# Attention and feed-forward on one core: first-layer products of the mean in four pieces, key pieces shared between two engines, first keys loaded ahead of the second weights

## The chip, the cores and the metric

The kernel runs on 1 core of one Trainium2 chip. Its engines work side by side, each through its own list of instructions in order: TensorE (PE, with its weight loads PEld), VectorE (DVE), ScalarE (ACT), GpSimd (POOL) and SyncE (SP), which here issues all DMAs. The metric is the device time of one execution in microseconds (us); lower is better.

## The reference

```python
B, C, Hh, Ww = (4, 128, 384, 32)            # q: (4, 12288, 128), kv: (4, 384, 32, 128)
kv_pool = kv.reshape(B, H // 4, 4, W // 4, 4, C).mean(axis=(2, 4))
k = v = kv_pool.reshape(B, -1, C) @ w_sr     # 768 keys per batch
s = scale * (q @ k.transpose(0, 2, 1))
a = exp(s - s.max(-1)); a /= a.sum(-1) + 1e-09
x = (a @ v).reshape(49152, 128)
h = x @ w_in                                 # 128 -> 2048
out = (h - tanh(h)) @ w_out                  # 2048 -> 128
```

The weights w_in and w_out are float64.

## The kernel before

The work is cut into 96 **groups** of 512 tokens, 24 for each of the 4 batches. The kernel does not compute the softmax directly: it works with the differences from the batch's mean key, for which expansions are exact enough, and a branch behind it computes everything plainly if that does not hold for the inputs.

Per batch, `keys` loads the keys in 12 pieces of 512 KB, sums each window of 16 (on POOL as four folds, L363, or on DVE as one reduction, L369), takes the mean (L391 to L396), shifts the keys by it, and multiplies with w_sr. `about_centre` multiplies the mean with w_in (**first**, L475: 16 products of one column, two passes each), takes h on DVE, and computes there from it, in some twenty short steps on 16 columns (L483 to L515), value, slope and third-order factor of the activation. From these it makes the value (L519), the matrix A of slopes (L602), the scaled w_in (`winr`) and the scaled w_out (`Wr`, by POOL, L607).

Per group, `attention` has 6 score products, in three tiles (L649), their exponentials less 1 and less s (ACT L653, DVE L656, tile r2), the sum of shares (L669), the sum of values (L673, L678), and dl, the result on DVE (L688), rounded on POOL to dr. `feed_forward` has 16 products **forth** (L726, in 8 tiles), a square on ACT and a cube on DVE (L730, L733; for one or two of the 8 tiles a copy on ACT and three steps on POOL, L737 to L744, tile rp) and 16 products **back** (L766) with the straight product (L715) into one accumulator, and ACT's copy with the value added (L772), which is stored.

At the start the float64 weights are turned into float32 by `words_of`: a load, three ACT steps and four DVE steps (L257, L260, L264, L276) for each of 4 parts of w_in and of w_out. `fits` computes at the end the flag for the branch: limits from h and the weights (L797 to L822), then the comparison with the shares (L835 to L852).

PSUM holds a ring of three **big** tiles (scores, forth and some others), one accumulator **acc**, and one **x** bank, which all the small products and the sums of attention take in turn.

The order of every engine's list is fixed when the kernel is built: each operation has a step number (its priority) and an assumed duration, and `Plan.run` places them one after the other in a time of its own; where an engine can begin several, the lowest step goes first. So a changed step or duration moves instructions all through the program.

Of the kernel before, what the change touches and what calls it, by code (L numbers as in the profile page):

```python
# [20 lines left out]
P = 128  # L21
KB = 64
# [124 lines left out]
def attention_then_ffn(ctx: ExitStack, tc: tile.TileContext, q, kv, w_sr, w_in, w_out, out):  # L147
# [18 lines left out]
    BUFS = {"kc": 2, "kvp": 1, "kTr": 2, "vv32": 1, "vvr": 2, "Mn": 2, "A": 2, "Wg": 2, "Wr": 2,  # L166
            "winr": 2, "q": 4, "qr": 3, "E": 2, "r2": 5, "t": 2, "dl": 2, "dr": 2, "u": 3, "r": 4,
            "rp": 2, "rs": 2, "v": 2, "z": 1, "o": 2, "row": 2, "col": 2, "G0": 2, "hb": 2, "W2": 1,
# [51 lines left out]
    WORDS = {"i": ("u", "u", "u", "E"), "o": ("E", "rs", "rs", "z")}  # L220

    def words_of(step, load_step, n, kind):
# [56 lines left out]
        plan.op(load_step, "SP", 0.5, load_words, (), (words,), late=2.0, dma=1.65)  # L279
# [8 lines left out]
    def weights(step, load_step):  # L288
# [3 lines left out]
        for n in range(NW):  # L292
            words_of(step + NW + n, load_step + 1 + n / 8, n, "o")
        for j in range(2):
            turned = f"turned.{j}"
            big(turned, step + 2 * NW + j)
            for k in range(2):
                def turn(j=j, k=k, turned=turned):
                    for f in range(8 * j + 4 * k, 8 * j + 4 * k + 4):
                        PE.matmul(out=plan[turned][:, (f % 8) * P : (f % 8 + 1) * P],  # L300
                                  lhsT=win32[:, f * P : (f + 1) * P], rhs=ident,
                                  start=True, stop=True)

                plan.op(step + 2 * NW + j, "PE", 1.0, turn, (("win32", 2 * j + k), "ident"),
                        ((turned, k),), late=0.2)
# [4 lines left out]
            plan.op(step + 2 * NW + j, "ACT", 1.03, copy, (turned,), (("winT", j),), late=0.1)  # L310
# [29 lines left out]
    def keys(b, s0):  # L340
# [7 lines left out]
        for j in range(NK):  # L348
            gap = 11 if b else 0.1
# [7 lines left out]
            plan.op(s - 8, "SP", 0.5, load, (), (key,), late=2.0, dma=1.65)  # L357
            if b or j % 3 == 2:
# [22 lines left out]
        for x, at in ((pc, s0), (pm, s3), (p4, s4)):  # L381
            bank(x, "x", at)
        big(pk, s1)
# [25 lines left out]
        def product():  # L409
            for c in range(2):  # L410
                PE.matmul(out=plan[pk][:, c * G : c * G + KH], lhsT=wsr,
                          rhs=plan[kvp][:, c * KH : (c + 1) * KH], start=True, stop=True)
# [5 lines left out]
        def product_by_key():  # L418
            for n in range(KT):
# [7 lines left out]
        def small_values():  # L427
            V.tensor_scalar(out=plan[vvr].rearrange("p k c -> p (k c)"), in0=plan[pv][:, 0:K],  # L428
                            scalar1=1.0 / (W * K), scalar2=None, op0=ALU.mult)
# [16 lines left out]
        plan.op(s1, "PE", 1.2, product, ("wsr", kvp), (pk,), late=0.2)  # L446
        plan.op(s1, "ACT", 0.9, copy_keys, (pk,), (kTr,), late=0.1)
        plan.op(s2, "PE", 1.75, product_by_key, ("wsr", kvp), (pv,), late=0.2)
        plan.op(s2, "ACT", 0.85, copy_values, (pv,), (vv32,), late=0.1)
        plan.op(s2, "DVE", 0.9, small_values, (pv,), (vvr,))  # L450
# [4 lines left out]
    def about_centre(b, s0):  # L455
# [11 lines left out]
        by = 4 if b else 1  # L467
        s1, s2, s3, s4, s5 = (s0 + n * by for n in range(1, 6))
        bank(ph, "x", s0 if b else s0 - 9.5)
        bank(pg, "x", s2 if b else s5 + 2)  # L470
        bank(pa, "x", s5 if b else s1 - 0.5)

        def first(n):
            for f in range(4 * n, 4 * n + 4):
                PE.matmul(out=plan[ph][:, f : f + 1], lhsT=win32[:, f * P : (f + 1) * P],  # L475
                          rhs=plan[cen], start=True, stop=True)
# [4 lines left out]
        def take():  # L481
            h, z = x(0), x(1)
            V.tensor_scalar(out=h, in0=plan[ph][:, 0:FT], scalar1=1.0, scalar2=None, op0=ALU.mult)  # L483
            V.tensor_tensor(out=z, in0=h, in1=h, op=ALU.mult)

        def first_order():
            h, z, p, g0, g1, a3, slope, y, inv = (x(n) for n in range(9))
            V.tensor_scalar(out=p, in0=z, scalar1=17.0 / 315, scalar2=-2.0 / 15, op0=ALU.mult,
# [28 lines left out]
        def value(n):  # L517
            for f in range(4 * n, 4 * n + 4):
                PE.matmul(out=plan[pg][:, 0:1], lhsT=wout32[:, f], rhs=x(3)[:, f : f + 1],  # L519
                          start=(f == 0), stop=(f == FT - 1))  # L520

        def copy_value():
            V.tensor_scalar(out=plan[G0], in0=plan[pg][:, 0:1], scalar1=1.0, scalar2=None,  # L523
                            op0=ALU.mult)

        for n in range(4):
            plan.op(s0, "PE", 1.1, partial(first, n), (cen, ("win32", n)), ((ph, n),), late=0.2)
        plan.op(s0, "DVE", 0.5, take, (ph,), (hb,))
        plan.op(s0 + 0.1, "DVE", 1.6, first_order, (hb,), (hb, gg))
        plan.op(s0 + 0.2, "DVE", 1.6, slopes_of, (hb,), (hb, iv))  # L530
        plan.op(s0 + 0.3, "DVE", 1.6, third_order, (hb,), (hb, ("stat", b), a3s))
        for n in range(4):
            plan.op(s2 if b else s5 + 2, "PE", 1.0, partial(value, n), (gg, ("wout32", n)), (pg,), late=0.2)
        plan.op(s2, "DVE", 0.12, copy_value, (pg,), (G0,))
        NW, FW = 4, FT // 4
        if b:
# [5 lines left out]
            plan.op(s0 + 1, "SP", 0.5, store_inverse, (iv,), (f"inverse.{b}",), late=2.5, dma=0.1)  # L542
            for j in range(2):
# [16 lines left out]
                plan.op(s0 + 1, "SP", 0.5, load_inverse, (f"inverse.{b}",), (ir,), late=2.5, dma=2.2)  # L560
                plan.op(s1 + j, "DVE", 2.2, scaled, (ir, "win32"), ((winr, j),), port=True)
        else:
            for j in range(2):
                pw = f"pw.{b}.{j}"
                big(pw, s1 + j * by / 2)
                for k in range(2):
                    dg = f"dg.{b}.{j}.{k}"
                    sb(dg, "Wg", [P, FW, C], step=s1 + j * by / 2 + k / 4)
# [14 lines left out]
                    plan.op(s1 + j * by / 2, *(("POOL", 1.25) if j else ("DVE", 1.1)), diagonal, (iv, "ident"), (dg,), port=True)  # L583
                    plan.op(s1 + j * by / 2, "PE", 0.9, scaled, (dg, "winT"), ((pw, k),), late=0.2)
# [4 lines left out]
                plan.op(s1 + j * by / 2, "ACT", 1.03, copy_scaled, (pw,), ((winr, j),), late=0.1)  # L589
        for n in range(NW):  # L590
            wg = f"wg.{b}.{n}"
            fs = slice(n * FW, (n + 1) * FW)
            sb(wg, "Wg", [P, FW, C], step=s3 + n / 4)

            def by_first(n=n, wg=wg, fs=fs):
                by = x(4)[:, fs].unsqueeze(2).to_broadcast([P, FW, C])
                (PL if b or n % 2 else V).tensor_tensor(out=plan[wg], in0=wout32[:, fs], in1=by, op=ALU.mult)

            def slopes(n=n, wg=wg):
                for k in range(FW):  # L600
                    f = n * FW + k
                    PE.matmul(out=plan[pa][:, 0:P], lhsT=winT[:, f], rhs=plan[wg][:, k],  # L602
                              start=(f == 0), stop=(f == FT - 1))

            def by_third(fs=fs):
# [3 lines left out]
            plan.op(s3 + n / 4, *(("POOL", 1.25) if b or n % 2 else ("DVE", 1.15)), by_first,  # L609
                    (gg, ("wout32", n)), (wg,), port=True)  # L610
            plan.op(s5, "PE", 1.1, slopes, (wg, "winT"), (pa,), late=0.2)
            plan.op(s4 + n / 4, "POOL", 1.25, by_third, (a3s, ("wout32", n)), ((Wr, n),))

        def copy_slopes():
            A.copy(out=plan[Am], in_=plan[pa][:, 0:P])

        plan.op(s5, "ACT", 0.3, copy_slopes, (pa,), (Am,), late=0.1)

    def attention(g, s0):
# [17 lines left out]
        plan.op(s0 - 10, "SP", 0.5, load_q, (), (qs,), late=2.0, dma=1.1)  # L637
# [68 lines left out]
    def feed_forward(g, s0):  # L706
# [7 lines left out]
        def straight():  # L714
            PE.matmul(out=plan[acc], lhsT=plan[Am], rhs=plan[dl], start=True, stop=False)  # L715
# [308 lines left out]
```

## Time and profile before

| | us |
|---|---|
| median of 3 runs | 1448.57 (1446.36 to 1449.13) |
| the profiled execution | 1445.03 |
| its span | 1443.3 |
| mean granted TensorE clock in it | 0.987 of full speed |

The profile is of one execution. Busy times are those of each engine; a matmul's end is modelled, so overlapping products count once, and a busy PE may still be slow. A stage is a stretch of the span; the last numbers of its row are the granted clock, the share of the DMA engines and GB/s. In brackets behind an instruction stands how long its engine was idle before it, and what ended that.

### The profile page before, as it was taken

Reading aid. Unit: us, or ns where it says so; the run is one execution under the profiler, and the core shown is the slowest. Engines: PE = TensorE matmul, PEld = TensorE weight load, DVE = VectorE, ACT = ScalarE, POOL = GpSimd, SP = SyncE. Lnnn points to the kernel's source line nnn. Section 1 sums busy time; section 2 is a strip of 40 time slices with the busy share of each in tenths; the row PEclk is TensorE's granted clock in tenths of the full one; section 3 lists DMA queues with packets and bytes.
Section 4 is the critical chain, followed back from the end, with each engine's and each line's share of the span. In section 5 each row is a group of like instructions: output and inputs, shape, how many; then the busy total and the mean of one; then the engine's idle time right before and its main releaser. Section 6 shows DMA issues by size and latency. Waiting matters only on the chain.

```text
span 1443.3 us, 17354 instructions
## 1 busy us (share of the span) xinstructions
PE 1388.8 (96%) x5814; PEld 1037.2 (72%) x5814; DVE 1208.5 (84%) x1216; ACT 1156.1 (80%) x1298; POOL 1102.8 (76%) x821
## 2 busy tenths in 40 slices
PE   2999999999999999999999999999999999999996
PEld 2777777777777777777777777777777777777773
DVE  7678888888888888888788888888878888888887
ACT  5468888876788888886688888887778888888885
POOL 4699767769999778676999976776867867867854
PEclk7899999999999999999999999999999999999999
DMA  9222111012322110111323111110111111111000
GB/s 351 67 88 74 37 37 44 30 38 82 115 74 81 37 44 31 44 35 55 96 80 97 58 37 45 37 38 30 60 44 34 40 45 37 37 45 37 30 28 25
DMA packets 39505, 84.52 MB, mean 59 GB/s; under 512 B 5136, under 2 KB 7312, under 8 KB 39408
## 3 DMA queue, kind: packets, MB, share of 16 engines
q1 hardware_dynamic: 39408, 83.34, 17.6%
q8 instruction: 47, 0.77, 0.2%
q14 instruction: 50, 0.41, 0.1%
HBM read 57.93 MB, written 25.39 MB: 58 GB/s over the span
## 4 chain that ended last, share of the span: by engine, by line
PE 79%; POOL 11%; DVE 4%; DMA 3%; ACT 1%; issue 1%; SPq 1%; DVEq 0%; POOLq 0%; ACTq 0%
PE big L726 21%; PE acc L766 21%; PE x L678 8%; PE x L669 8%; PE big L649 8%; PE x L673 5%; PE acc L715 5%; POOL z L744 3%; POOL rp L744 3%; DVE r L733 2%; POOL z L740 1%; DMA kc<-in_kv_dram 1%; POOL kc L363 1%; PE x L475 1%; DVE winr L557 1%
## 5 line engine op out<-in xcount | busy, mean ns | idle before, releaser
L733 DVE SCALAR_TENSOR_TENSOR r<-big,u 128x1024 fp32r<-128x1024 f32 x624 | 751.9, 1219 | 131.0 <-ACT u L730 104.1
L730 ACT ACTIVATE u<-big 128x1024 f32<-128x1024 f32 x624 | 637.5, 1032 | 155.9 <-PE big L726 151.2
L726 PE MATMUL big<-dr,winr 128*128 128x512 f32 x1536 | 524.4, 423 | 6.8 <-DVE r L733 5.4
L766 PE MATMUL acc<-r,Wr 128*128 128x512 f32 x1248 | 405.4, 408 | 0.8 <-DVE r L733 0.8
L656 DVE SCALAR_TENSOR_TENSOR r<-E,big 128x1024 fp32r<-128x1024 f32 x288 | 349.5, 1214 | 51.6 <-ACT E L653 45.9
L726 PEld LDWEIGHTS big<-dr,winr 128*128 128x128 f32 x1536 | 278.6, 189 | 130.2 <-DVE r L733 40.5
L744 POOL TENSOR_TENSOR rp<-z,v 128x1024 fp32r<-128x1024 f32 x144 | 346.6, 2407 | 10.4
L744 POOL TENSOR_TENSOR z<-z,v 128x1024 f32<-128x1024 f32 x144 | 349.7, 2428 | 6.0
L740 POOL TENSOR_SCALAR z<-v 128x1024 f32<-128x1024 f32 x144 | 157.9, 1097 | 242.2 <-ACT v L737 238.5
L653 ACT ACTIVATE E<-big 128x1024 f32<-128x1024 f32 x288 | 296.8, 1032 | 30.5 <-PE big L649 29.6
L766 PEld LDWEIGHTS acc<-r,Wr 128*128 128x128 f32 x1248 | 234.4, 189 | 71.1 <-issue 18.2
L649 PE MATMUL big<-qr,kTr 128*128 128x512 f32 x576 | 185.8, 405 | 0.2 <-DVE vvr L428 0.2
L678 PE MATMUL x<-r,vvr 128*128 128x512 f32 x576 | 182.9, 399 | 0.0
L669 PE MATMUL x<-r,share 128*128 128x512 f32 x576 | 179.9, 398 | 1.4 <-DVE G L523 1.0
L737 ACT COPY v<-big 128x1024 f32<-128x1024 f32 x144 | 146.3, 1016 | 37.9 <-PE big L726 35.7
L669 PEld LDWEIGHTS x<-r,share 128*128 128x128 f32 x576 | 108.5, 189 | 30.3 <-DVE G L523 3.1
L678 PEld LDWEIGHTS x<-r,vvr 128*128 128x128 f32 x576 | 108.0, 188 | 28.0 <-issue 3.4
L649 PEld LDWEIGHTS big<-qr,kTr 128*128 128x128 f32 x576 | 104.4, 189 | 31.9 <-DVE r L733 7.4
L766 PE MATMUL acc<-rp,Wr 128*128 128x512 f32 x288 | 106.8, 452 | 4.1 <-POOL rp L744 4.0
L715 PE MATMUL acc<-dl,A 128*128 128x512 f32 x192 | 102.1, 613 | 3.7 <-ACT o L772 3.7
L673 PE MATMUL x<-q,Mn 128*128 128x512 f32 x192 | 98.1, 592 | 0.7 <-ACT t L682 0.7
L363 POOL TENSOR_TENSOR kc<-kc 128x512 f32<-128x512 f32 (+2 forms) x108 | 86.6, 803 | 10.4 <-DMA kc<-in_kv_dram 6.0
(133 smaller groups left out, 786.3 us busy)
## 6 DMA issues: line engine op xcount, KB each, us to landing
q<-in_q_dram SPq DMA_DIRECT2D x96, 256.0 KB
out_dram<-o SPq DMA_DIRECT2D x96, 256.0 KB
kc<-in_kv_dram SPq DMA_DIRECT2D x38, 512.0 KB
r<-in_kv_dram SPq DMA_DIRECT2D x8, 512.0 KB
kc<-inverse SPq DMA_DIRECT2D x6, 512.0 KB
u<-in_moe_w_in_dram SPq DMA_DIRECT2D x3, 512.0 KB
left<-t SPq DMA_DIRECT2D x96, 2.0 KB
rs<-in_moe_w_out_dram SPq DMA_DIRECT2D x2, 512.0 KB
```

Of the source, the lines that this page charges most:

```text
L649: PE.matmul(out=half(plan[s], h), lhsT=plan[kTr][:, n * P : (n + 1) * P], rhs=plan[qr], start=True, stop=True)
L653: A.activation(out=plan[e], in_=plan[s], func=AF.Exp)
L656: V.scalar_tensor_tensor(out=plan[r], in0=plan[e], scalar=-1.0, in1=plan[s], op0=ALU.add, op1=ALU.subtract)
L669: PE.matmul(out=plan[den], lhsT=share, rhs=half(plan[f"r2.{g}.{k}"], h), start=(n == 0), stop=(n == KT - 1))
L678: PE.matmul(out=plan[num], lhsT=plan[vvr][:, n], rhs=half(plan[f"r2.{g}.{k}"], h), start=False, stop=(n == KT - 1))
L715: PE.matmul(out=plan[acc], lhsT=plan[Am], rhs=plan[dl], start=True, stop=False)
L726: PE.matmul(out=half(plan[hp], h), lhsT=plan[winr][:, f * P : (f + 1) * P], rhs=plan[dr], start=True, stop=True)
L730: A.activation(out=plan[u], in_=plan[hp], func=AF.Square)
L733: V.scalar_tensor_tensor(out=plan[r], in0=plan[hp], scalar=1.0, in1=plan[u], op0=ALU.add, op1=ALU.mult)
L740: PL.tensor_scalar(out=plan[z], in0=plan[v], scalar1=1.0, scalar2=1.0, op0=ALU.add, op1=ALU.mult)
L744: PL.tensor_tensor(out=plan[to], in0=plan[x], in1=plan[y], op=ALU.mult)
L766: PE.matmul(out=plan[acc], lhsT=plan[Wr][:, f], rhs=half(plan[r], h), start=False, stop=(f == FT - 1))
```

## The change

1. **First products in pieces.** For later batches the 16 products of the mean with w_in are four pieces of 4, each with its own use of the x bank and its own DVE copy; the value and the slopes are split in the same way, and their parts are added on DVE. Steps that depend on them have new step numbers. In batch 0 all 16 go in one run into the acc bank, and group 0's straight product comes last instead of first.
2. **Key pieces.** In later batches every other piece is reduced on DVE instead of folded on POOL (`j % 2`); they are spaced by 9 steps instead of 11 and the key and mean stages begin 20 steps earlier.
3. **Start.** The loads and the turning of w_out stand behind the keys of batch 0. While these are summed, five products of the identity with 512 pooled keys (`warm`) run on PE; nobody reads their result. `vvr` of batch 0 is made by ACT; of the four tiles Wg for the slopes POOL makes all, where DVE made two.
4. **End.** The limits in `fits` stand at the step of the eighth group from the end; its sums and the comparison use the x bank.
5. The assumed transfer times are shorter (1.65 to 1.27, 1.1 to 0.65), and Wg has 4 buffers instead of 2.

```diff
-    BUFS = {... "Wg": 2 ...}
+    BUFS = {... "Wg": 4 ...}
-    WORDS = {"i": ("u", "u", "u", "E"), "o": ("E", "rs", "rs", "z")}
+    WORDS = {"i": ("u", "u", "u", "E"), "o": ("u", "u", "u", "z")}
...
-            words_of(step + NW + n, load_step + 1 + n / 8, n, "o")
+            words_of(out_step + n / 8, load_out + n / 8, n, "o")
...
-            gap = 11 if b else 0.1
+            gap = 9 if b else 0.1
...
-            if b or j % 3 == 2:
+            if (j % 2 if b else j % 3 == 2):
                 for k, w in enumerate((8, 4, 2, 1)):
...
+        if b == 0:
+            big("warm", s0 - 3)
+            for j in range(WN // KB - 1, NK):
+                def warm(j=j):
+                    PE.matmul(out=plan["warm"][:, 0:WN], lhsT=ident,
+                              rhs=plan[kvp][:, (j + 1) * KB - WN : (j + 1) * KB], start=True,
+                              stop=True)
+                plan.op(s0 - 3, "PE", 1.2, warm, ["ident"] + [(kvp, i) for i in range(j + 1)],
+                        ("warm",))
...
-        plan.op(s2, "DVE", 0.9, small_values, (pv,), (vvr,))
+        plan.op(s2 + (0 if b else 2), "DVE" if b else "ACT", 0.9, small_values, (pv,), (vvr,))
...
+        first_at = [s0 + 2 * n if b else s0 - 9.9 + n / 4 for n in range(4)]
+        known = s0 + 7 if b else s0 - 9
+        slopes_at = [s0 + 14 + 4 * n if b else n / 2 - SL for n in range(4)]
+        value_at = [s0 + 12 + 4 * n if b else n / 2 + VL for n in range(4)]
+        for n in range(4):
+            if b or n == 0:
+                bank(f"{ph}.{n}", "x" if b else "acc", first_at[n])
+            bank(f"{pg}.{n}", "x", value_at[n])
+            bank(f"{pa}.{n}", "x", slopes_at[n])
...
-        plan.op(s0, "DVE", 0.5, take, (ph,), (hb,))
+            plan.op(first_at[n], "PE", 0.9, partial(first, n), (cen, ("win32", n)),
+                    (f"{ph}.{n}" if b else (f"{ph}.0", n),), late=0.2)
+            if b:
+                plan.op(first_at[n], "DVE", 0.17, partial(take_first, n), (f"{ph}.{n}",), ((hb, n),))
+        if not b:
+            plan.op(first_at[3], "DVE", 0.17, partial(take_first, 0), (f"{ph}.0",), (hb,))
...
-                (PL if b or n % 2 else V).tensor_tensor(out=plan[wg], in0=wout32[:, fs], in1=by, op=ALU.mult)
+                PL.tensor_tensor(out=plan[wg], in0=wout32[:, fs], in1=by, op=ALU.mult)
...
+                if n:
+                    V.tensor_tensor(out=plan[Am], in0=of, in1=plan[Am], op=ALU.add)
+                else:
+                    A.copy(out=plan[Am], in_=of)
...
-            PE.matmul(out=plan[acc], lhsT=plan[Am], rhs=plan[dl], start=True, stop=False)
+            PE.matmul(out=plan[acc], lhsT=plan[Am], rhs=plan[dl], start=(g > 0), stop=(g == 0))
...
-        big("of_sums", step - 4)
-        big("of_left", step)
+        bank("of_sums", "x", early + 2)
+        bank("of_left", "x", step)
...
-    weights(-LEAD - 50, -LEAD - 60)
+    weights(-LEAD - 50, -LEAD - 60, -LEAD - 29.7, -LEAD - 46)
...
-        keys(b, first - LEAD - (60 if b else 40))
-        about_centre(b, first - LEAD - (40 if b else 30))
+        keys(b, first - LEAD - (80 if b else 40))
+        about_centre(b, first - LEAD - (60 if b else 30))
...
-    fits((NGT - 1) * UN - 4)
+    fits((NGT - 8) * UN, (NGT - 1) * UN - 4)
```

On SP, at the very start, the loads of w_out (L238) stood between those of w_in (L236) and of the first keys (L355):

```order
 L236 DMA u<-in_moe_w_in_dram 128x1024 x3
 L236 DMA E<-in_moe_w_in_dram 128x1024
-L238 DMA E<-in_moe_w_out_dram 128x4x256
-L238 DMA rs<-in_moe_w_out_dram 128x4x256 x2
-L238 DMA z<-in_moe_w_out_dram 128x4x256
-L355 DMA r_101<-in_kv_dram 128x1024
+L355 DMA r_93<-in_kv_dram 128x1024
 L355 DMA r<-in_kv_dram 128x1024
 L355 DMA rp<-in_kv_dram 128x1024
 L355 DMA kc<-in_kv_dram 128x1024
```

They now follow behind the twelfth key piece and the first load of q.

On DVE, behind the last of the short steps of batch 0 (L515 before), stood these rows (L574 and L597 make Wg, L656 are the score tiles, L733 is a cube):

```order
L515 TENSOR_TENSOR hb<-hb 128x16
L574 TENSOR_TENSOR Wg<-ident,hb 128x512 x2
L391 TENSOR_REDUCE row<-kvp 128x4
L688 TENSOR_TENSOR dl<-x,t 128x512
L597 TENSOR_TENSOR Wg<-wout_69,hb 128x512
L656 SCALAR_TENSOR_TENSOR r_456<-E,big 128x1024
L656 SCALAR_TENSOR_TENSOR r_466<-E,big 128x1024
L597 TENSOR_TENSOR Wg<-wout_69,hb 128x512
```

Now these rows follow the last short step (L692 are the score tiles, L369 reduces pieces of batch 1, L607 makes Wg, L401 sums rows, L264 to L276 turn w_out, L724 is dl; between L724 and r_466 come r_443 and one more L369):

```order
L692 SCALAR_TENSOR_TENSOR r_356<-E,big 128x1024
L692 SCALAR_TENSOR_TENSOR r_363<-E,big 128x1024
L369 TENSOR_REDUCE kvp<-kc 128x64
L692 SCALAR_TENSOR_TENSOR r_374<-E,big 128x1024
L607 TENSOR_TENSOR Wg<-ident,hb 128x512 x2
L401 TENSOR_REDUCE row<-kvp 128x4
L369 TENSOR_REDUCE kvp<-kc 128x64
L264 SCALAR_TENSOR_TENSOR wout_69<-u,v 128x512
L257 TENSOR_SCALAR v<-v 128x512
L276 ISA wout_69<-wout_69,o 128x1024
L260 TENSOR_SCALAR v<-v 128x512
L724 TENSOR_TENSOR dl<-x,t 128x512
```

The first group's score tiles and the turning of w_out moved behind the short steps, ahead of the first dl.

On PE, in the key stage of batch 1, the products of the mean were one run of 16 (32 passes):

```order
L766 MATMUL acc<-r,Wr 128x512 x2
L475 MATMUL x<-col,win_67 128x1 x16
L726 MATMUL big<-dr,winr 128x512 x2
L649 MATMUL big<-qr,kTr 128x512 x2
L726 MATMUL big<-dr,winr 128x512 x2
```

Now they are pieces of 4, of which these are the first two:

```order
L763 MATMUL big<-dr,winr 128x512 x2
L499 MATMUL x<-col,win_67 128x1 x4
L803 MATMUL acc<-r,Wr 128x512 x2
L763 MATMUL big<-dr,winr 128x512 x2
L803 MATMUL acc<-r,Wr 128x512 x2
L499 MATMUL x<-col,win_67 128x1 x4
L763 MATMUL big<-dr,winr 128x512 x2
```

Three pairs of full width stand between the first and the second piece; the third and fourth follow a group later.

166 lines of the change are left out of this document (93 added, 73 removed).

## The prediction

> **What bounds the kernel now.** I read the page first, then busy times by stage, then the chain and the order of time. The page's rows of the engines and of TensorE's slices:
>
> ```profile
> PE 1388.8 (96%) x5814; PEld 1037.2 (72%) x5814; DVE 1208.5 (84%) x1216; ACT 1156.1 (80%) x1298; POOL 1102.8 (76%) x821
> PE   2999999999999999999999999999999999999996
> ```
>
> PE has work nearly always, except in the first and the last slice. The stages (start, end, length, then busy time of PE, PEld, DVE, ACT, POOL, and the granted clock) show how much is open there:
>
> ```profile
> 0.00:33.20 33.20, 6.35 (x32) 5.50 (x32) 26.46 (x48) 17.27 (x27) 12.55 (x22) 0.79 0.97 369
> 33.20:41.10 7.90, 6.92 (x27) 5.63 (x28) 0.76 (x4) 1.74 (x2) 5.25 (x7) 0.57 0.13 51
> 41.10:65.80 24.70, 21.43 (x132) 18.32 (x131) 19.46 (x37) 11.39 (x14) 17.61 (x24) 0.93 0.32 97
> 65.80:92.40 26.60, 24.88 (x113) 18.54 (x114) 15.90 (x16) 15.87 (x19) 24.48 (x21) 1.00 0.20 60
> 400.00:1400.00 1000.00, 993.79 (x4091) 740.81 (x4089) 855.96 (x818) 837.01 (x934) 777.83 (x552) 0.99 0.15 48
> 1400.00:1443.30 43.30, 30.46 (x119) 19.20 (x117) 30.75 (x36) 21.71 (x24) 17.98 (x10) 0.96 0.09 30
> ```
>
> From 400 to 1400 us PE is idle for 6 us in all, so no wait is left there to speak of. What can be won is the start (PE works 6 of the first 33 us), the tail (13 us idle of 43), and any time in which PE is busy but slow. The last kind shows in PE's order of time around the key stage of batch 2 (start, length, line, operation, count):
>
> ```profile
> 657.88 0.63 PE L726 MATMUL big<-dr,winr 128*128 128x512 f32 x2
> 658.35 0.62 PE L766 MATMUL acc<-r,Wr 128*128 128x512 f32 x2
> 658.80 4.61 PE L475 MATMUL x<-col,win 128*128 128x1 f32 x32
> 663.27 1.20 PE L726 MATMUL big<-dr,winr 128*128 128x512 f32 x2
> 664.27 1.05 PE L649 MATMUL big<-qr,kTr 128*128 128x512 f32 x2
> 665.13 1.05 PE L726 MATMUL big<-dr,winr 128*128 128x512 f32 x2
> 1005.89 3.64 PE L475 MATMUL x<-col,win 128*128 128x1 f32 x32
> ```
>
> A pair of 512 columns starts 0.47 us after the one before it ahead of the first-layer products (657.88 to 658.35), and 0.86 us behind them (664.27 to 665.13). The stages cut at the products and behind them show why:
>
> ```profile
> 314.80:318.30 3.50, 3.50 (x33) 3.47 (x32) 3.00 (x3) 0.79 (x1) 2.50 (x3) 1.00 0.02 5
> 318.30:325.00 6.70, 6.70 (x27) 4.66 (x27) 5.55 (x21) 4.83 (x6) 2.04 (x2) 1.00 0.12 41
> 658.80:661.20 2.40, 2.40 (x24) 2.40 (x22) 2.40 (x3) 0.77 (x1) 2.20 (x3) 1.00 0.00 0
> 661.20:668.00 6.80, 6.80 (x22) 5.83 (x23) 2.74 (x10) 2.86 (x3) 2.04 (x2) 0.50 0.00 0
> 1009.40:1012.80 3.40, 3.40 (x10) 2.72 (x10) 1.31 (x8) 2.17 (x3) 1.63 (x2) 0.50 0.00 0
> ```
>
> After 32 passes of one column in a row the granted clock is 0.50 for 6.8 us in batch 2 and for 3.4 us in batch 3; in batch 1 it stays at 1.00. PE is never idle in these stages.
>
> **Term 1, the clock: -4.7 us.** At half clock a pair takes 0.86 instead of 0.47, so 6.8 + 3.4 = 10.2 us hold 10.2 x 0.47 / 0.86 = 5.6 us of work: 4.6 to 4.7 us lost. The change issues these products in four pieces, 8 passes each (0.9 us at 3.64 / 32 = 0.114 a pass), with pairs between them. The nearest two pieces are three pairs (1.4 us) apart, so any 3.5 us hold at most 1.8 us of one-column work or little more; in batch 1 even 3.5 us in a row passed without a fall. I take the whole loss as won. Bounds: 0 (it falls all the same) and -8 (other executions may fall in all three batches).
>
> The Trainium skill ("TensorE: Matmul & The Clock Gate", Part 1) gives half clock after at least one idle window of about 3.4 us. By that rule a busy PE keeps its clock, the split would bring nothing, and the sum would be 4.7 us worse. The rows here speak against it: the clock fell while PE was busy throughout.
>
> **Term 2, the start: -4.5 us.** Rows of time around the first keys:
>
> ```profile
> 26.51 2.85 POOL L363 TENSOR_TENSOR rp<-rp 128x512 f32<-128x512 f32 x3 [0.64 <-DMA rp<-in_kv_dram]
> 30.26 2.52 POOL L363 TENSOR_TENSOR r<-r 128x512 f32<-128x512 f32 x3 [0.53 <-DMA r<-in_kv_dram]
> 33.93 0.59 PE L403 MATMUL x<-row,wsr 128*128 128x1 f32 x2 [17.64 <-DVE row L396]
> 34.77 1.87 PE L475 MATMUL x<-col,win 128*128 128x1 f32 x8 [0.25 <-DVE col L406]
> 46.47 0.17 DVE L483 TENSOR_SCALAR hb<-x 128x16 f32<-128x16 f32 x1
> 52.50 0.18 DVE L515 TENSOR_TENSOR hb<-hb 128x16 f32<-128x16 f32 x1
> 65.85 0.73 PE L726 MATMUL big<-dr,winr 128*128 128x512 f32 x2 [0.32 <-DVE r L656]
> ```
>
> POOL waits twice for key pieces three loads apart: (30.26 - 26.51) / 3 = 1.25 us per 512 KB. The four loads of w_out now stand behind the keys, so the last piece lands 4 x 1.25 = 5.0 us earlier, at 25.2, and the mean could reach PE at 28.9 instead of 33.93. Five warming products stand ahead of it on PE. Their price, and those of the steps below:
>
> ```profile
> 1387.74 0.86 PE x L673 x2
> L369 DVE TENSOR_REDUCE kvp<-r 128x64 f32<-128x1024 f32 x6 | 7.2, 1206 | 0.0
> L656 DVE SCALAR_TENSOR_TENSOR r<-E,big 128x1024 fp32r<-128x1024 f32 x288 | 349.5, 1214 | 51.6 <-ACT E L653 45.9
> L574 DVE TENSOR_TENSOR Wg<-ident,hb 128x512 f32<-128x512 f32 x2 | 2.1, 1106 | 0.0
> L276 DVE CUSTOM_DVE_ANT_0 wout<-wout,o 128x1024 uint16<-128x1024 uint16 x4 | 2.7, 685 | 0.0
> L257 DVE TENSOR_SCALAR v<-v 128x512 f32<-128x512 f32 x8 | 3.5, 433 | 4.6 <-ACT v L254 4.6
> L363 POOL TENSOR_TENSOR kc<-kc 128x512 f32<-128x512 f32 (+2 forms) x108 | 86.6, 803 | 10.4 <-DMA kc<-in_kv_dram 6.0
> ```
>
> A warming product has the shape of L673: 0.86 us at full clock, 1.7 at half. They run as the pieces are summed, the last not before 28.1; I put the mean's product at 30 (bounds 28.9 and 31.5). Then 0.5 us to the column on DVE and all 32 passes in one run, 3.6 us at full clock: h is complete at about 34.5 instead of 46.47 (at half clock, 0.234 a pass by L475's 1.87 / 8, at 38).
>
> But this lead of 12 us is mostly eaten on DVE, which used to have w_out finished by now. Its small steps took 52.68 - 46.47 = 6.2 us before; with three w_out steps among them (0.69 + 0.43 + 0.43) they end at about 42.5 instead of 52.7. On PE the first forth product stands behind the shares of tile r_466. Up to that tile DVE's new order has five subtractions and three key reductions at 1.21 (9.7), two Wg at 1.1, a row sum of 0.3, four w_out steps (two of 0.69, two of 0.43) and a dl of 0.7: 9.7 + 2.2 + 0.3 + 2.2 + 0.7 = 15.1. The vvr scaling has gone to ACT and is not among them. So the first forth is at 42.5 + 15.1 + 0.9 (hops, and one pair on PE) = 58.5, 7.3 us earlier than 65.85. It has less behind it: the 32 slope passes (3.6) and one pair of scores (0.5) come later, so 7.3 - 4.1 = 3.2 us are won. Between 65.8 and 92.4 PE also waited 26.60 - 24.88 = 1.7 us beside a POOL that was busy 24.48; with half the folds gone from POOL I count 1.3 of them as won: -4.5. On SP the w_out loads pass behind the keys and one q load; they land from 27 to 33, ahead of the DVE steps that read them, and q is needed only with the keys. What covers the w_out steps is gone: each 0.7 us more on DVE here is 0.7 us on the end. Bounds: 0 (POOL's Wr waits for w_out's third part, and dr behind it) and -9 (clock up at once, w_out's steps in gaps).
>
> **Term 3, the tail: -4 us.** DVE sets the pace after the last attention. There lie:
>
> ```profile
> 1404.56 0.83 DVE L803 TENSOR_REDUCE tops<-big 128x5 f32<-128x640 f32 x1 [1.73 <-PE big L797]
> 1411.08 0.96 DVE L814 TENSOR_SCALAR row<-row 128x4 f32<-128x4 f32 x1
> 1412.22 2.28 DVE L819 TENSOR_SCALAR row<-row 128x4 f32<-128x4 f32 x1
> 1414.41 0.22 DVE L822 TENSOR_SCALAR row<-tops 128x4 f32<-128x4 f32 x1
> 1423.87 0.73 PE L726 MATMUL big<-dr,winr 128*128 128x512 f32 x2 [2.10 <-DVE r L733]
> ```
>
> L814 to L822 run from 1411.08 to 1414.41 + 0.22, 3.6 us with L811 ahead of them some 3.7, and L803 is 0.8; all of it moves some seven groups earlier, where DVE is idle for 14% of the time (855.96 of 1000). The long L819 stays long or gets short, hidden either way. The of_left tile leaves the ring of three big tiles, which frees forth sooner. 4.5 us leave DVE; 4 of them count. Bounds -2 (PE's later backs waited for POOL's rp anyway) and -5.
>
> **Term 4, later key pieces and the shared bank: 0.** 18 pieces move from POOL's folds (86.6 us for 36 pieces: 2.4 each, and a short last one) to one DVE reduction of 1.21: 21.8 us more on an engine with 144 us free in that stretch. The many short DVE steps behind 318.3 did not make PE wait (6.70 of 6.70). The x bank gets 12 short uses per later batch instead of 3, each with a DVE read; a wait of 0.1 for each new one would be 2.7 us, the relief of POOL about as much back. Bounds -3 and +6.
>
> **Sum.** -4.7 - 4.5 - 4 + 0 = -13.2. The profiled execution took 1445.03 us (its span 1443.3 and 1.7 around it): 1431.8. The median of the runs shown is 3.5 us above it, which may be clock falls as well; 1448.57 - 13.2 is 1435.4. I say 1434.
>
> **Rivals.** (1) The start brings nothing, since DVE with w_out's steps, and POOL's Wr behind them, hold the first forth and the backs to the old pace: 1434 + 4.5 = 1438.5. For it: DVE has 19.5 of 24.7 us busy from 41 to 66 already. Chance 0.15. (2) The clock falls with the four pieces as well, or does not depend on them: 1434 + 4.7 = 1439. Against it: it fell twice right in or behind these products and in no other place between 92 us and the last products. The Trainium skill's page, with idle time as the cause, is on this side. Chance 0.10. (3) Slower: the 18 reductions each stand ahead of a subtraction or cube that PE's next product needs, and the three big tiles come free late. Each can cost PE its 1.21 us, 21.8 in all: 1434 + 21.8 = 1456. It cancels the gain at 0.73 us each and is slower by a measurable amount from 0.9 us each. Against it: 318.3 to 325. Chance 0.05. (4) The start wins twice as much and the clock fell in three batches in most runs: 1434 - 4.5 - 3.3 = 1426. Chance 0.10. My forecast: 0.60.
>
> **How the numbers follow.** 0.2% is 2.9 us, about what a measurement of this kernel can tell from no change. Cases (1), (2) and (4) stay below 1445; if two of the bad ones meet, with term 4 near its upper bound, the gain is gone: 0.08 for no change, 0.05 for slower, 0.87 for faster. Range 1423 to 1444: from below case (4) to beyond (1) and (2), most of term 4's bound in it.
>
> **What would show it.** Clock: 1.00 in all three later key stages, and pairs 0.47 apart behind the one-column pieces. Start: last key fold begins at about 25.2, h complete at 34 to 38, first forth product at 58 to 59, DVE busy without a gap from 40. Tail: no DVE row of limits among the last cubes, and some 4 us less from the last dl to the end. Wrong it would be if PE shows new idle time behind key reductions, or if the first output leaves later than about 86 us.

## The result, and the profile after

The changed kernel takes 1458.07 us (median of 4 runs, 1457.55 to 1460.10) against 1448.85 us for the kernel before in the same comparison. The ratio is 1.0069, 95% interval 1.0052 to 1.0087: it is slower by 0.7%, where 1434 us were forecast. The profiled execution took 1457.55 us, with a span of 1455.8.

Page of the changed kernel, TensorE's busy time, its slices and its clock:

```profile
PE 1401.2 (96%) x5824; PEld 1044.2 (72%) x5824; DVE 1246.4 (86%) x1264; ACT 1159.2 (80%) x1299; POOL 1056.8 (73%) x751
PE   5899999989999999989999999998999999999996
PEclk8999999999999999999999999999999999999998
```

PE starts earlier (5 and 8 in the first two slices, where it had 2 and 9), but three later slices (from 291, 619 and 983 us) have lost a tenth, and PE as a whole is busy 12 us longer with nearly the same work. Where did the time go? The table gives the start of ACT's copy of a group's output (L772 before, L812 after), less the same in the kernel before, worked out from these rows of the traces, in us; e_dve_cube, e_tail and e_best are cured kernels of the experiments below. Each row compares two single executions, and that of the kernel before is among its fastest (1445.03 against a median of 1448.85):

| group | 10 | 30 | 55 | 80 | 92 | 95 |
|---|---|---|---|---|---|---|
| after | -5.3 | +1.3 | +4.8 | +12.1 | +14.6 | +12.6 |
| e_dve_cube | -4.1 | -2.3 | -3.4 | -2.4 | +0.1 | -2.2 |
| e_tail | -5.0 | -3.5 | -5.0 | -3.9 | -1.4 | -9.0 |
| e_best | -4.7 | -3.4 | -4.7 | -4.5 | -2.1 | -9.7 |

So the start has won 5.3 us, and each of the three later key stages (they lie between the columns 10 and 30, 30 and 55, 55 and 80) loses 3.5 to 7.3. Between groups 80 and 92, where the limits now stand, all four kernels lose 2.4 or 2.5 more. The stages in which the clock fell, in the changed kernel (columns as in the prediction):

```profile
302.40:309.20 6.80, 5.54 (x21) 5.16 (x22) 5.72 (x8) 2.06 (x3) 2.62 (x3) 0.50 0.08 31
654.00:660.80 6.80, 6.09 (x22) 5.56 (x23) 5.72 (x7) 2.31 (x3) 2.62 (x3) 0.50 0.00 0
1005.50:1012.40 6.90, 6.90 (x28) 6.10 (x26) 5.08 (x8) 2.56 (x4) 2.62 (x3) 0.51 0.00 0
1432.20:1439.00 6.80, 5.17 (x12) 3.67 (x13) 4.99 (x7) 3.12 (x4) 2.60 (x2) 0.50 0.10 39
```

Half clock for 6.8 us in all three key stages and in the tail. Just ahead of the first of them, PE in order of time (start, length, line, operation, and in brackets the idle time before it and what ended that):

```profile
299.10 0.62 PE L763 MATMUL big<-dr,winr 128*128 128x512 f32 x2
303.66 1.22 PE L685 MATMUL big<-qr,kTr 128*128 128x512 f32 x2 [3.94 <-DVE r L770]
```

PE waits 3.94 us for a cube of DVE. DVE in the same microseconds, then POOL:

```profile
297.24 0.16 DVE L536 TENSOR_SCALAR hb<-hb 128x16 f32<-128x16 f32 x1
297.43 2.38 DVE L537 TENSOR_TENSOR hb<-hb 128x16 f32<-128x16 f32 x1
299.85 0.17 DVE L538 TENSOR_TENSOR hb<-hb 128x16 f32<-128x16 f32 x1
300.06 2.20 DVE L539 TENSOR_TENSOR hb<-hb 128x16 f32<-128x16 f32 x1
302.30 0.17 DVE L540 TENSOR_TENSOR hb<-hb 128x16 f32<-128x16 f32 x1
302.39 1.22 DVE L770 SCALAR_TENSOR_TENSOR r<-big,u 128x1024 fp32r<-128x1024 f32 x1
```

```profile
296.25 1.05 POOL L777 TENSOR_SCALAR z<-v 128x1024 f32<-128x1024 f32 x1 [1.19 <-ACT v L774]
297.39 2.40 POOL L781 TENSOR_TENSOR z<-z,v 128x1024 f32<-128x1024 f32 x1
299.86 2.37 POOL L781 TENSOR_TENSOR rp<-z,v 128x1024 fp32r<-128x1024 f32 x1
```

L537 to L540 have one form and one size, yet two of them take 0.17 us and two take 2.38 and 2.20. The long ones end at 299.81 and 302.26, and POOL's cube steps end at 299.79 and 302.23. The short one, L538, starts at 299.85, between POOL's two instructions. This is no matter of one place: in all 14 traces together, 192 of the steps with two inputs or TENSOR_SCALAR that write the tiles hb and row last 0.3 us or longer, and every one of them ends within 0.04 us of the end of a POOL instruction. Two more steps are long in the same way beside POOL's Wg (L524 0.90, L525 0.96). In each of the three stages 5.8 us are lost so on DVE (0.90 + 0.96 + 2.38 + 2.20 less 4 x 0.17). In the kernel before, the last of these steps ran while POOL waited for them (its row there, with the idle time ahead of it):

```profile
325.77 3.04 POOL L607 TENSOR_TENSOR Wr<-wout,hb 128x512 fp32r<-128x512 f32 x3 [3.64 <-DVE hb L515]
```

The new step numbers put a cube of POOL beside them.

The tail shows the same thing, in the steps of the comparison:

```profile
1426.37 0.95 DVE L885 SCALAR_TENSOR_TENSOR row<-row 128x4 f32<-128x4 f32 x1
1427.35 0.16 DVE L886 TENSOR_TENSOR row<-row 128x4 f32<-128x4 f32 x1
1427.55 2.23 DVE L887 SCALAR_TENSOR_TENSOR row<-row 128x4 f32<-128x4 f32 x1
1429.82 0.16 DVE L889 TENSOR_TENSOR row<-row 128x4 f32<-128x4 f32 x1
1430.02 2.19 DVE L890 TENSOR_TENSOR row<-row 128x4 f32<-128x4 f32 x1
```

PE, behind them:

```profile
1433.83 2.35 PE L763 MATMUL big<-dr,winr 128*128 128x512 f32 x4 [4.57 <-DVE r L770]
```

### The profile page after: what moved, and what is told of

It reads as the page before. It is cut to its first block, busy times and chain, and to the rows that moved or that the text cites. A ratio compares the mean times of both kernels' runs of the same rounds, so it can differ in the third digit from the quotient of the medians.

```text
span 1455.8 us, 17448 instructions
## 1 busy us (share of the span) xinstructions
PE 1401.2 (96%) x5824; PEld 1044.2 (72%) x5824; DVE 1246.4 (86%) x1264; ACT 1159.2 (80%) x1299; POOL 1056.8 (73%) x751
## 4 chain that ended last, share of the span: by engine, by line
PE 84%; DVE 8%; POOL 4%; DMA 2%; ACT 1%; issue 1%; SPq 0%; DVEq 0%; POOLq 0%; ACTq 0%
PE big L763 23%; PE acc L803 22%; PE x L714 8%; PE big L685 8%; PE x L705 8%; PE x L709 5%; PE acc L751 5%; DVE r L770 3%; POOL rp L781 1%; DVE r L692 1%; POOL z L781 1%; PE x L544 1%; POOL z L777 1%; PE x L634 1%; DMA rp<-in_kv_dram 1%
## 5 line engine op out<-in xcount | busy, mean ns | idle before, releaser
L763 PE MATMUL big<-dr,winr 128*128 128x512 f32 x1536 | 525.6, 425 | 13.7 <-DVE r L770 10.9
L692 DVE SCALAR_TENSOR_TENSOR r<-E,big 128x1024 fp32r<-128x1024 f32 x288 | 349.8, 1215 | 47.8 <-ACT E L689 44.3
L714 PE MATMUL x<-r,vvr 128*128 128x512 f32 x576 | 186.5, 405 | 0.0
L803 PEld LDWEIGHTS acc<-rp,Wr 128*128 128x128 f32 x288 | 54.0, 189 | 30.7 <-issue 17.3
```

The costliest lines, as they stand in the source:

```text
L692: V.scalar_tensor_tensor(out=plan[r], in0=plan[e], scalar=-1.0, in1=plan[s], op0=ALU.add, op1=ALU.subtract)
L714: PE.matmul(out=plan[num], lhsT=plan[vvr][:, n], rhs=half(plan[f"r2.{g}.{k}"], h), start=False, stop=(n == KT - 1))
L763: PE.matmul(out=half(plan[hp], h), lhsT=plan[winr][:, f * P : (f + 1) * P], rhs=plan[dr], start=True, stop=True)
L803: PE.matmul(out=plan[acc], lhsT=plan[Wr][:, f], rhs=half(plan[r], h), start=(g == 0 and f == 0), stop=(g > 0 and f == FT - 1))
```

## The experiments

Theory **A**: DVE's short steps wait for POOL's running instruction, PE idles behind them, and the clock falls. Rivals: **B**, the pieces and their many uses of the x bank hold PE; **C**, the key reductions on DVE hold PE (the prediction's third rival). Times are medians, ratios are against the kernel before on the same chip.

**e_halves.** POOL's long instruction is cut in two.

```diff
-                PL.tensor_tensor(out=plan[to], in0=plan[x], in1=plan[y], op=ALU.mult)
+                for h in range(2):
+                    PL.tensor_tensor(out=half(plan[to], h), in0=half(plan[x], h),
+                                     in1=half(plan[y], h), op=ALU.mult)
```

> Each product of POOL's cubes (L781, 1024 columns, 2.40 us) is issued as two of 512 columns. Theory A (DVE's 16-column steps of two operands last until POOL's running instruction ends; behind them PE stands 4.1 us and the clock falls): L537 and L539 last at most 1.3 us instead of 2.38 and 2.20, PE's gap behind them falls from 4.1 to about 2 us, and the time to 1445-1452 us. Theory B (four pieces of the one-column products and their joins hold PE) and theory C (the key reductions on DVE hold PE): the gap stays 4.1 us and the time at 1457-1460.

Measured: 1457.9 us, ratio 1.0066 (1.0046 to 1.0086). DVE in order of time:

```profile
297.54 1.28 DVE L537 TENSOR_TENSOR hb<-hb 128x16 f32<-128x16 f32 x1
298.85 1.22 DVE L538 TENSOR_TENSOR hb<-hb 128x16 f32<-128x16 f32 x1
300.10 1.19 DVE L539 TENSOR_TENSOR hb<-hb 128x16 f32<-128x16 f32 x1
301.32 1.18 DVE L540 TENSOR_TENSOR hb<-hb 128x16 f32<-128x16 f32 x1
```

The steps follow the length of POOL's instruction, as A says: half as long an instruction, half as long a step. The expected time was wrong: one step passes between two instructions of POOL, and with twice as many instructions four steps are held instead of two. 4 x 1.2 us are as much as 2.38 + 0.17 + 2.20 + 0.17. PE's gap stayed at 3.88 us. So gap and time came out as B and C had them; only the length of DVE's steps speaks for A here, and the next three runs have to decide.

**e_behind, e_dve_cube, e_other_cube.** The first leaves the cube on POOL, but behind the short steps. The second makes it on DVE and ACT like most others. The third makes three other cubes there, two groups later.

```diff
+                behind = [(f"Wr.{b + 1}", 0)] if (g, n) in ((16, 0), (40, 0), (64, 0)) else []
-                plan.op(s, "POOL", 1.05, moved_pool, (v,), (z,))
+                plan.op(s, "POOL", 1.05, moved_pool, [v] + behind, (z,))
```

```diff
-            if n in ON_POOL[g % 2]:
+            if n in ON_POOL[g % 2] and (g, n) not in ((16, 0), (40, 0), (64, 0)):
```

> In each of the three later key stages POOL's cube that ran beside the 16-column steps (group 16, 40 and 64, first piece) waits for the first Wr, which waits for the last of these steps. A: L537 and L539 last 0.17 us each, though the four Wg ahead of them can hold one or two others by 0.9; PE's gap of 4.1 us is gone or under 1.5, the clock stays at 1.00 in these stages, 1436-1447 us. B and C: nothing of theirs is changed, the gap or one like it stays, and the later cube can only cost: 1457 or more.

> The same three cubes are made by DVE and ACT like the other cubes, so POOL runs no cube there, and DVE has 1.22 us more in each stage. A: as above, 1436-1447 us. B: 1457-1460. C (DVE short of time because of the key reductions): slower than the changed kernel, 1459-1463.

> The changed kernel with three other cubes of POOL given to DVE and ACT: those of groups 18, 42 and 66 (first piece), two groups behind the ones that ran beside the 16-column steps. The same work leaves POOL as in the kernel with groups 16, 40 and 64 (1442.1 us). A (the place matters, the 16-column steps stay beside POOL's cube): L537 and L539 stay at 2.38 and 2.20, PE's idle time of 4 us stays, 1455-1460 us. If it was POOL's relief that won there: 1441-1447.

Measured: e_behind 1447.23 us, 0.9987 (0.9969 to 1.0005); e_dve_cube 1442.13 us, 0.9957 (0.9938 to 0.9976); e_other_cube 1477.32 us, 1.0192 (1.0156 to 1.0227). A step of e_dve_cube, and a stage behind it:

```profile
299.41 0.17 DVE L537 TENSOR_TENSOR hb<-hb 128x16 f32<-128x16 f32 x1
...
299.00:309.00 10.00, 9.38 (x48) 7.12 (x48) 9.61 (x16) 6.03 (x8) 4.63 (x5) 1.00 0.55 165
```

L537 is back at 0.17 us in both cured kernels; in e_dve_cube the idle time of 3.94 has shrunk to 0.69 and the clock stays at 1.00 in all three stages. In e_other_cube L537 stays at 2.38 in batch 1, the idle time stays at 3.89 to 3.95 in all three, and a new one comes (below). So it is the place of the cube beside the short steps that makes PE wait, not POOL's load. In e_behind and e_dve_cube the pieces, their joins and the key reductions are all still there, so neither B nor C explains the gap. e_behind gains less because its later cube meets the scaling of w_in:

```profile
302.78 5.48 DVE L590 TENSOR_TENSOR winr<-win,kc 128x1024 fp32r<-128x1024 f32 x2
309.45 0.79 PE L763 MATMUL big<-dr,winr 128*128 128x512 f32 x1 [2.12 <-DVE r L770]
```

My expectation for the time of e_other_cube missed by 17 us, so its time decides nothing. Its trace shows where it went: a key piece that is loaded late holds the head of DVE's queue, and the cubes behind it. This is a risk of reducing keys on DVE that the prediction did not name; in the changed kernel itself the only such wait of a later batch is 0.97 us (340.17).

```profile
345.53 1.22 DVE L369 TENSOR_REDUCE kvp<-kc 128x64 f32<-128x1024 f32 x1 [5.41 <-DMA kc<-in_kv_dram]
```

**e_port.** The planner already knows operations that exclude POOL's work (`port=True`); the short steps were not marked.

```diff
-        plan.op(known, "DVE", 1.8, first_order, (hb,), (hb, gg))
+        plan.op(known, "DVE", 1.8, first_order, (hb,), (hb, gg), port=b > 0)
...
```

> The planner is told that the three runs of 16-column steps of batches 1 to 3 and POOL's work exclude each other, as it is told for the larger two-operand steps; no instruction is added or left out. A: if the order so made keeps them apart on the chip too, no 16-column step is longer than 0.3 us and the time is 1435-1446; where steps of 0.9 us and more stay, the gap stays in proportion. B and C: 1456-1460, as only places move.

Measured: 1454.49 us, 1.0034 (1.001 to 1.0059). The plan keeps them apart in its own time, the chip only partly, since nothing but the order is fixed:

```profile
296.62 1.04 DVE L535 TENSOR_SCALAR hb<-hb 128x16 f32<-128x16 f32 x1
297.57 0.16 DVE L536 TENSOR_SCALAR hb<-hb 128x16 f32<-128x16 f32 x1
297.76 2.38 DVE L537 TENSOR_TENSOR hb<-hb 128x16 f32<-128x16 f32 x1
```

With L524 (0.90) 3.8 us are lost on DVE in a stage instead of 5.8, and PE's idle time there is 2.11 us instead of 3.94: roughly in proportion. The clock still falls in all three stages, and the time alone lies close to what B and C had. e_behind, with an order held by a real dependence, does better.

**e_tail.** On top of e_dve_cube, the cube beside the comparison goes to DVE too.

```diff
-            if n in ON_POOL[g % 2] and (g, n) not in ((16, 0), (40, 0), (64, 0)):
+            if n in ON_POOL[g % 2] and (g, n) not in ((16, 0), (40, 0), (64, 0), (94, 3)):
```

> On top of the three cubes on DVE: the last cube but one of POOL (group 94, second of its two), which ran beside the comparison's steps at the end, goes to DVE and ACT as well. If POOL's running instruction is what makes L885, L887 and L890 last 0.95, 2.25 and 2.19 us, they last about 0.2, PE's idle time of 4.6 us behind them falls to at most 1.5, the clock stays up there, and the time is 1436-1440 us (5 us less on DVE, 1.2 more for the cube). If these steps are long by themselves, the cube only adds: 1442-1444.

Measured: 1436.26 us, 0.9888 (0.9864 to 0.9912). DVE there, in order of time:

```profile
1412.63 0.16 DVE L885 SCALAR_TENSOR_TENSOR row<-row 128x4 f32<-128x4 f32 x1
1412.83 0.16 DVE L886 TENSOR_TENSOR row<-row 128x4 f32<-128x4 f32 x1
1413.03 0.16 DVE L887 SCALAR_TENSOR_TENSOR row<-row 128x4 f32<-128x4 f32 x1
```

**e_one_run** asks for the clock alone: on top of e_dve_cube, the products of the mean are one operation with one bank again.

```diff
+        def first_all():
+            for n in range(4):
+                first(n)
...
+                plan.op(first_at[3], "PE", 3.6, first_all, (cen, "win32"), (f"{ph}.0",), late=0.2)
```

> On top of the kernel with the three cubes on DVE (1442.1 us, ratio 0.9957): the first-layer products of batches 1 to 3 in one run of 32 passes and one bank, as in the kernel before; the rest stays. If such a run by itself lowers the clock (term 1 of the prediction), the granted clock is 0.50 for 3.4 to 6.8 us behind it in at least one of the three batches though PE is never idle for over 1 us there, and the time is 1443-1448 us. If only idle time lowers it, the clock stays at 1.00 and the time at 1441-1443. If the pieces' joins cost PE something (theory B), it is below 1441.

Measured: 1449.01 us, 0.9976 (0.996 to 0.9992). PE at the run in batch 1, then stages at and behind it:

```profile
267.81 3.63 PE L499 MATMUL x<-col,win 128*128 128x1 f32 x32
...
269.40:270.40 1.00, 1.00 (x11) 1.00 (x11) 1.00 (x1) 0.00 (x0) 1.00 (x1) 1.00 0.00 0
270.40:271.40 1.00, 1.00 (x11) 1.00 (x11) 0.12 (x1) 0.00 (x0) 0.83 (x2) 1.00 0.00 0
271.40:275.40 4.00, 3.70 (x11) 2.46 (x11) 3.51 (x14) 1.98 (x3) 1.85 (x2) 0.57 0.00 0
```

The clock falls behind the run in all three batches (0.53 from 620.0 to 623.4 and 0.67 from 966.8 to 970.2), with PE busy ahead of it in the first two and idle for 0.6 of the 3.4 us ahead in the third; in e_dve_cube, with four pieces, it stays at 1.00. The table's rows would put the cost at 1.2 to 2.0 us a batch (from group 10 to 30, 30 to 59 and 59 to 80 this kernel loses 3.4, 1.9 and 1.2 us against the kernel before, e_dve_cube 1.8, 0.7 and -0.8), of which some 0.5 can be its own held short steps. In whole times the intervals of the two ratios overlap, but the mean clock of each of the ten executions of e_one_run (0.982 to 0.988) is below that of each of the ten of e_dve_cube (0.989 to 0.993). So the sign is shown by the clock and its size only about. B, which had the time below 1441, gets no support: without the joins nothing is won.

**e_keys_pool.** All key pieces of the later batches go back to POOL, on top of e_dve_cube.

```diff
-            if (j % 2 if b else j % 3 == 2):
+            if b or j % 3 == 2:
```

> On top of the three cubes on DVE: all key pieces of batches 1 to 3 folded on POOL, as in the kernel before. C (18 key reductions hold PE): 1432-1440 us. If the reductions fit into DVE's free time and relieve POOL (2 to 2.5 us a batch won in the changed kernel between the stages): 1446-1452 us.

Measured: 1455.61 us, 1.0021 (1.0009 to 1.0034). C falls: without the 18 reductions the kernel is slower, by 9 us by the ratios and 13 by the spans (1454.0 against 1441.2). It is also slower than the 1446 to 1452 expected. Why POOL with all the pieces costs so much in the changed order (9 steps apart, 20 earlier) is shown only in part: POOL is busy for 1079.2 us, less than the 1102.8 of the kernel before, but folds (L363) stand between two of its cubes from 141.10 to 144.75, and PE then waits 0.95 us for the second (151.25).

**e_wr_first, e_best.** The first Wr stands ahead of the four Wg on POOL, so that these begin behind the short steps; alone on top of e_dve_cube, and on top of e_tail.

```diff
-            plan.op(slopes_at[n], "POOL", 1.25, by_first, (gg, ("wout32", n)), (wg,), port=True)
+            plan.op(slopes_at[n], "POOL", 1.25, by_first,
+                    [gg, ("wout32", n)] + ([a3s] if b else []), (wg,), port=True)
-        third_at = [s0 + 15 + 4 * n if b else s0 + 2 + n / 4 for n in range(4)]
+        third_at = [s0 + (15 + 4 * n if n else 7.5) if b else s0 + 2 + n / 4 for n in range(4)]
```

> On top of the three cubes on DVE: in batches 1 to 3 the first Wr stands ahead of the four Wg on POOL, so these begin behind the last 16-column step. A: L524 to L526 last 0.17 us each instead of 0.90, 0.96 and 0.96 (2.3 us less on DVE in each stage), PE's gap of 0.85 behind them is gone, the time is 1438-1442 us: 0.9 a batch, more if the clock or later waits hang on it. If nothing waits for DVE there any more, 1442.

> The changed kernel with all three cures: the four cubes (groups 16, 40, 64, and the second of 94) on DVE and ACT, and the first Wr ahead of the Wg on POOL. No 16-column step behind the start and no step of the comparison longer than 0.3 us, no idle time of PE over 1.5 us from 100 us on, clock 1.00 from 60 us to the last cubes. If the gains add (1.6 us for the Wr's place, by the runs on their own), 1434-1436 us; if the Wr's place wins nothing beside the rest, 1436-1438.

Measured: e_wr_first 1440.57 us, 0.9917 (0.9892 to 0.9941); e_best 1435.83 us, 0.9885 (0.9867 to 0.9903). No short step of the later batches is longer than 0.3 us any more, but beside e_tail the Wr's place wins nothing that can be measured. e_best beats both kernels. From 400 to 1400 us PE is idle less than 8 us, and the clock is full:

```profile
400.00:1400.00 1000.00, 992.24 (x4103) 739.15 (x4102) 865.86 (x848) 838.13 (x933) 726.95 (x497) 1.00 0.14 46
```

**e_limits_late, b_tail.** The limits go back to their old place, with the four cubes of e_tail on DVE; and the kernel before gets the same cure at its own tail.

```diff
-    fits((NGT - 8) * UN, (NGT - 1) * UN - 4)
+    fits((NGT - 1) * UN - 12, (NGT - 1) * UN - 4)
```

```diff
-            if n in ON_POOL[g % 2]:
+            if n in ON_POOL[g % 2] and (g, n) not in ((94, 0), (94, 3)):
```

> The changed kernel with the four cubes on DVE and ACT, and the limits back at the place where they were before the change. If 4.5 us less of DVE's work in the tail is worth 4 us (term 3 of the prediction): 1439-1442 us. If the limits lie beside other work at the old place too, or if at the new place they cost as much between groups 87 and 89: 1435-1438.

> The kernel before, with both of POOL's cubes of group 94 made by DVE and ACT; these ran beside the steps of its limits and comparison (0.96, 2.28, 1.90). 4.6 us less waiting on DVE against 2.4 us more for two cubes: 1444-1448 us, ratio 0.997 to 1.000. If the cure alone were what wins and the change only lost, it would stand near the cured changed kernel, at 1438 or below.

Measured: e_limits_late 1440.96 us, 0.9922 (0.99 to 0.9945), 4.7 us more than e_tail, with intervals that overlap a little; b_tail 1445.46 us, 0.9957 (0.9938 to 0.9977). At their old place two steps of the limits are held again, by the cube of group 94 that is still on POOL:

```profile
1404.31 2.28 DVE L856 TENSOR_TENSOR row<-row 128x4 f32<-128x4 f32 x1
...
1406.65 2.37 DVE L862 TENSOR_SCALAR row<-tops 128x4 f32<-128x4 f32 x1
```

So the cure wins something in the kernel before as well; against that kernel, cured at its tail, the change with its own cures is some 10 us faster.

## Why the prediction was wrong

**The steps that failed.** Two sentences carried the mistake. Term 4: "The many short DVE steps behind 318.3 did not make PE wait (6.70 of 6.70)". That held at the place where the steps stood then, beside a POOL that was mostly idle (one of them, L498, was held for 0.50 us there); the change moved them, and the term went on using the old price. Term 3: "The long L819 stays long or gets short, hidden either way". L819's row (2.28 us, beside L822 of the same width at 0.22), with L814's (0.96), was the sign of the mechanism, and I did not ask what made them long: in the trace of before both end within 0.1 us of a cube step of POOL. The bounds of term 4, -3 and +6, left out this price. The runs put in its place: 14.6 us for the three cubes beside the key stages (spans 1455.8 to 1441.2) and 6.8 us for the one in the tail (1441.2 to 1434.4), 21.4 of the 23.6 us by which the profiled execution missed 1434. These gains are those of moving the cubes, which moves other work and spares the clock too. That the two numbers are so close is partly chance, as the other terms below did not come out one by one.

The Trainium skill ("SBUF — State Buffer", section "Who interferes with whom") has the rule: VectorE and GpSimd share one pair of ports, whoever issues first keeps it for the whole instruction, and the other blocks; it names VectorE's operations with two inputs in SBUF, and `tensor_scalar` in its two-port modes. The rows agree: a step of 0.17 us lasts 2.38 beside POOL's 2.40. Weighed against L819 in the prediction, this rule would have asked where the change puts the short steps.

**Term 1, the clock: mechanism right, sum wrong.** A run of 32 passes lowered the clock in 8 of the 9 key stages of the three kernels that have it (before, b_tail, e_one_run), and the four pieces of e_dve_cube did not lower it in any. They are not safe everywhere: in e_keys_pool it fell for 6.8 us at 77.8, with PE busy for 3.27 of the 3.4 us before, in which two pieces of 8 one-column passes stood and a third began (the products for the value, L544); what lowered it there no run isolates. But "I take the whole loss as won" left out that the clock has a second way to fall. At the pair times of the prediction 6.8 us at half clock cost 3.1 us, and the changed kernel has four such stretches. From group 10 to 80 it is at half clock for 20.4 us, the kernel before for 10.2; the term had expected none. The Trainium skill's rule of the idle window ("TensorE: Matmul & The Clock Gate", Part 1), which I set against the one-column runs as if only one could hold, agrees with these falls, behind 3.94 and 4.57 us of idle time, though at 302.4 the clock fell when PE had been idle for 2.7 us. It does not explain those behind PE's busy runs, nor does a window of 3.4 us quite fit e_behind, where 2.12 us of idle time come before 0.56. Both causes are there.

**Term 2, the start: right, one step of it by luck.** -5.3 us at group 10, against -4.5. In the runs with the same start it is -4.1 to -8.1, and it goes with the length of the stretch at half clock that begins between 42 and 47 us: 6.8 us go with -4.1 to -5.0, 3.4 us with -5.2 to -6.2, none with -8.0 and -8.1 (e_keys_pool, with other key work, left out). The steps came where they were put:

```profile
24.19 2.53 POOL L363 TENSOR_TENSOR r<-r 128x512 f32<-128x512 f32 x3 [0.73 <-DMA r<-in_kv_dram]
32.93 0.17 DVE L504 TENSOR_SCALAR hb<-acc 128x16 f32<-128x16 f32 x1 [0.40 <-PE acc L499]
58.05 0.63 PE L763 MATMUL big<-dr,winr 128*128 128x512 f32 x2
```

The last fold begins at 24.19 (said 25.2), h is taken at 32.93 (34.5), the first forth is at 58.05 (58.5). But the way there was another: DVE's short steps ended at 39.8 (said 42.5), and DVE, said to be busy throughout, then waited for PE ahead of dl:

```profile
53.34 0.69 DVE L724 TENSOR_TENSOR dl<-x,t 128x512 f32<-128x512 f32 x1 [3.74 <-PE x L714]
```

**Term 3, the tail: net size right once cured, its parts not.** Moving the limits is worth 4.7 us (e_limits_late against e_tail; said 4). This is the difference of two larger numbers. Behind group 92 the move wins 8.1 us (from the copy of group 92 to that of 95, e_limits_late takes 39.3 us and e_tail 31.2). At the new place the limits are not hidden, as the term had it: from group 80 to 92 the runs that moved them take 163.3 us or a little more, the kernel before and e_limits_late 160.8. PE has next to no idle time there, and the limits bring 12 passes on PE (1.3 us); where the rest goes is not shown. And the 4.7 holds beside a comparison that is not held; in the changed kernel L885 to L890 lose 4.9 us, and PE waits 4.57 where it had waited 2.10. And part of the limits' 3.6 us was waiting for POOL from the start: L814 and L819 take 3.2 us together where 0.3 would do.

**Term 4, the shared bank and the key pieces.** It was put at 0, and in the cured kernels something costs nearly 5 us. From group 10 to 80 e_best takes 1006.3 us at full clock, the kernel before 1006.1, of which by the pair times 4.6 were lost to the clock. So the 4.7 us of term 1 were won and went again. PE is idle for 10.5 us there instead of 8.3; where the rest goes, and whether the x bank has a part in it, stays open. The joins of the first products hardly do: e_one_run, without them, loses 4.8 us more than e_dve_cube on this way, about what its 10.2 us at half clock cost. That the reductions cost nothing was too modest: in the new order they win 9 us against POOL's folds (e_keys_pool).

**The rivals.** Slower was given 0.05, by a mechanism that did not occur (the reductions); that its 1456 lies near the measured 1458.07 is chance. The true mechanism had no place in the sum. With the cures the time is near the forecast, 1435.83 against 1434 us, but by the table's rows not term by term: e_best wins 4.7 to group 10 (said 4.5), loses 0.2 from 10 to 80 (said 4.7 won), loses 2.4 from 80 to 92 (said nothing), and wins 7.6 behind (said 4). So the agreement is in part luck.

## What to carry to other kernels

In these runs a short VectorE step of the kinds listed below costs what it takes alone only if GpSimd is idle; beside a long GpSimd instruction it costs what is left of that one, and a chain of such steps pays again for each instruction. So when a change moves a chain of short steps, look up what GpSimd does at the new place, and hold the order with a dependence, since a planner's time is not the chip's. A row that is ten times as long as its neighbour of the same size is a question to settle before the sum is made.

## What the runs showed of the hardware

- Which steps are held: two inputs in SBUF (16 columns 2.38 us, 4 columns 2.19), but also one input, TENSOR_SCALAR on 16 columns (L535 of e_port 1.04) or 4 columns (L862 of e_limits_late 2.37). Not held: steps that read PSUM (dl 0.68 us everywhere), TENSOR_REDUCE (L369 1.21), and one column (L817 of the kernel before, 0.15). RECIPROCAL is not held either: in e_one_run it begins 0.20 us behind POOL's step of 2.43 us and takes its usual 0.25:

```profile
624.84 0.25 DVE L530 RECIPROCAL hb<-hb 128x16 f32<-128x16 f32 x1
...
624.64 2.43 POOL L785 TENSOR_TENSOR rp<-z,v 128x1024 fp32r<-128x1024 f32 x1
```

- It works both ways: beside the two L590 of e_behind (5.48 us), POOL's steps take 2.65 instead of 1.05 and 3.91 instead of 2.40:

```profile
303.85 2.65 POOL L777 TENSOR_SCALAR z<-v 128x1024 f32<-128x1024 f32 x1
306.58 3.91 POOL L781 TENSOR_TENSOR z<-z,v 128x1024 f32<-128x1024 f32 x1
```

- The granted clock fell to 0.50 behind idle times of PE from 2.11 us on (e_port), and behind 32 one-column passes without idle time. Idle times of 2.10 (before, 1421.77) and 2.19 us (e_keys_pool, 366.20) did not lower it, nor, from 60 us on in all traces, did one shorter than 2 us by itself. Its stretches at half clock in the key stages last 3.4, 6.8 or 13.7 us, so close to whole multiples of 3.4.
